# Linear-attention block with a dense expert layer on one core: key sums turned round, numerators kept transposed, denominators taken apart

## The chip, the cores and the metric

The kernel runs on one core of a Trainium2 chip. The metric is the device time of one execution in microseconds (us). Names of engines: PE is TensorE's matmul stream and PEld its weight loads, DVE is VectorE, ACT is ScalarE, POOL is GpSimd, SP is SyncE, which issues most of the transfers (DMAs).

## The reference, cut to what matters

All numbers are fp32. There are 2048 tokens of 512 features, 32 heads of 16 features, and 8 experts of 1792 hidden features.

```python
x = A_x
h = x + attention(layernorm(x))            # A
out = h + experts(layernorm(h))            # B

# attention: per head, features are two softmaxes of a small projection
phi_q = concat([softmax(pq), softmax(-pq)])        # 32 features a head
phi_k = concat([softmax(pk), softmax(-pk)])
kv  = einsum("bhsf,bhsd->bhfd", phi_k, v)          # sum over all tokens
z   = einsum("bhsf->bhf", phi_k)                   # sum over all tokens
num = einsum("bhqf,bhfd->bhqd", phi_q, kv)
den = einsum("bhqf,bhf->bhq", phi_q, z)[..., None] + 1e-6
o   = (num / den) @ wo

# experts: all 8 are used by every token (top 8 of 8), weighted by a softmax gate
h_  = gelu(einsum("nd,edf->nef", xt, w1))
y   = einsum("nef,efd->ned", h_, w2)
out = einsum("ne,ned->nd", cw, y)
```

The features phi_q and phi_k of a head are non-negative, and kv and z are needed in full before the first query can be answered.

## The kernel before, in words

Tokens are cut into 16 tiles of 128 (NT). A table STAGES lists stages as (lag, function); in step i, the stage with lag l works on tile i - l. The functions of one step are written in the order of the table, and the recording layer then sets the order of each engine's instructions from all of them; buffers are handed out by pools, so an instruction also waits for the last user of its buffer. SBUF pools are s4 (43 slots of 4 KB a partition) and s2 (13 slots of 2 KB); PSUM has 4 banks named ps and 4 named pacc.

For a tile of keys: x_stats and x_norm (layer norm: statistics on DVE, the power -0.5 on POOL, the subtraction and scaling on DVE, L157), x_trans (four PE transposes, L162), k_proj (two projections with the split fp32r product of L66 to L68, three matmuls for one), k_exp and k_feat (the softmaxes: maxima and minima L175 and L176, sums L182, reciprocals L183 on DVE, products L184 on POOL), and k_sum (L231). k_sum takes eight matmuls: the features of four heads (128) are the stationary operand, and the values of these heads with a column of ones behind each (4 x 17 = 68 columns) are the moving one. The sums of all tiles stay in two pacc banks. After the last tile keys_done (L272) masks the parts that belong to other heads.

For a tile of queries: q_proj, q_sub, q_exp, q_feat as above, q_trans (eight transposes, L262), q_num (L284: eight matmuls with the transposed features stationary and the 68 columns of kv moving, then on DVE the addition of 1e-6 L288, the reciprocal L289 and the product L290, all straight from PSUM), q_otrans (four transposes and the split into two fp32r parts), q_out (projection, residual, statistics of the second norm), q_norm, q_ntrans, and the gate: gate_parts (L333) multiplies with the gate weights in four column tiles of 32 side by side, chosen by tile_position.

From step END + 1 on, the expert layer is fed in between: hook runs four pieces of moe a step. Each quad there uses the four ps banks (L66 to L68 with ps), each down the pacc banks. From about 345 us to the end the expert layer alone fills PE.

Two lines carry the key sums and the numerators:

```python
nc.tensor.matmul(kvp[b][:, i * HN:(i + 1) * HN], phi[:, g * P:(g + 1) * P], v[:, g * HG:(g + 1) * HG, :]...)
nc.tensor.matmul(p[:, i * HN:(i + 1) * HN], phT[:, b * n + i, :], kv[:, b * n + i, :], start=True, stop=True)
```

## Time and profile before

| what | value |
|---|---|
| time, median of three runs | 2473.61 us (2472.48 to 2475.82) |
| time of the profiled execution | 2476.47 us |
| its span, first to last instruction | 2474.8 us |
| granted TensorE clock, mean | 0.995 |
| PE busy | 2449.9 us (99%) |
| DVE busy | 2159.9 us (87%) |
| ACT busy | 1757.4 us (71%) |
| POOL busy | 493.0 us (20%) |

The profile comes from one execution. "Busy" of PE is the union of the modelled spans of its matmuls, which overlap; how fast PE goes is therefore read from the starts of groups that follow each other, not from busy time or from the mean of one.

### The profile page before, as it was taken

The numbers are of one execution on the slowest core, as the hardware profiler recorded it, in microseconds if no ns is written. First come the engines' busy times: TensorE is split into PE (matmuls) and PEld (weight loads), VectorE is DVE, ScalarE is ACT, GpSimd is POOL, SyncE is SP. The second block draws the span as 40 slices with busy tenths as digits, with TensorE's granted clock in tenths as the row PEclk, the third lists the DMA queues.
The fourth block names the chain that finished last, engine by engine and source line by source line (L and its number), as shares of the span: only waits on it lengthen the run. The fifth ranks groups of instructions, "written<-read, shape, count | busy, mean of one in ns | idle before, by whom it ended". The sixth has DMA issues, their size and how long they took to land.

```text
span 2474.8 us, 32087 instructions
## 1 busy us (share of the span) xinstructions
PE 2449.9 (99%) x11272; PEld 2033.7 (82%) x11272; DVE 2159.9 (87%) x3204; ACT 1757.4 (71%) x2886; POOL 493.0 (20%) x562
## 2 busy tenths in 40 slices
PE   9999999999999999999999999999999999999998
PEld 8888778888888888888888888878888888888886
DVE  7677898988989989889896998889989889898987
ACT  4344477777777777777776777677777777777774
POOL 4565101111111111111111331111111111111120
PEclk9999999999999999999999999999999999999999
DMA  3001348787787787877877898887877887877785
GB/s 112 10 26 56 116 171 170 141 169 159 146 158 152 159 168 142 168 160 137 167 151 188 184 189 160 209 184 162 150 159 147 164 162 141 167 155 158 155 155 143
DMA packets 175202, 369.22 MB, mean 149 GB/s; under 512 B 15136, under 2 KB 81696, under 8 KB 175040
## 3 DMA queue, kind: packets, MB, share of 16 engines
q0 software_dynamic: 62304, 204.50, 49.6%
q1 hardware_dynamic: 111680, 162.62, 20.6%
q8 instruction: 88, 1.44, 0.2%
q14 instruction: 74, 0.61, 0.1%
q10 hardware_dynamic: 1056, 0.05, 0.0%
HBM read 158.38 MB, written 216.60 MB: 152 GB/s over the span
## 4 chain that ended last, share of the span: by engine, by line
PE 89%; DVE 4%; DMA 1%; issue 1%; POOL 1%; ACT 0%; SPq 0%; DVEq 0%; POOLq 0%; ACTq 0%
PE ps L66 15%; PE ps L67 15%; PE ps L68 15%; PE pacc L67 14%; PE pacc L68 14%; PE pacc L66 14%; PE ps L284 1%; DMA out_dram<-s 1%; DVE s L61 1%; DVE s L182 1%; PE pacc L162 1%; PE pacc L262 0%; POOL s L184 0%; DVE s L604 0%; DMA s<-in_B_w_dram 0%
## 5 line engine op out<-in xcount | busy, mean ns | idle before, releaser
L61 DVE TENSOR_TENSOR s<-s,s 128x512 fp32r<-128x512 f32 (+1 forms) x800 | 755.6, 958 | 158.7 <-ACT s L60 148.8
L60 ACT ACTIVATE s<-s 128x512 fp32r<-128x512 f32 (+1 forms) x800 | 669.7, 843 | 23.8 <-DVE s L511 8.7
L66 PE MATMUL pacc<-s,s 128*128 128x512 f32 x1732 | 678.1, 392 | 2.9 <-ACT s L60 2.9
L67 PE MATMUL pacc<-s,s 128*128 128x512 f32 x1732 | 675.7, 390 | 0.6 <-DVE s L61 0.6
L68 PE MATMUL pacc<-s,s 128*128 128x512 f32 x1732 | 675.6, 390 | 0.0
L66 PE MATMUL ps<-s,s 128*128 128x512 f32 x1664 | 652.3, 392 | 8.8 <-DVE ps L656 3.1
L67 PE MATMUL ps<-s,s 128*128 128x512 f32 x1664 | 649.2, 390 | 0.5 <-DVE s L61 0.5
L68 PE MATMUL ps<-s,s 128*128 128x512 f32 x1664 | 649.1, 390 | 0.0
L541 ACT ACTIVATE s<-pacc 128x512 f32<-128x512 f32 x742 | 440.2, 595 | 191.8 <-PE pacc L68 166.9
L603 ACT ACTIVATE ps<-ps 128x512 f32<-128x512 f32 x448 | 262.7, 587 | 190.3 <-DVE ps L656 119.0
L66 PEld LDWEIGHTS pacc<-s,s 128*128 128x128 f32 x1732 | 326.0, 188 | 71.9 <-ACT s L60 3.3
L67 PEld LDWEIGHTS pacc<-s,s 128*128 128x128 f32 x1732 | 326.1, 188 | 68.7 <-DVE s L61 1.9
L68 PEld LDWEIGHTS pacc<-s,s 128*128 128x128 f32 x1732 | 326.1, 188 | 68.0
L66 PEld LDWEIGHTS ps<-s,s 128*128 128x128 f32 x1664 | 313.1, 188 | 77.4 <-DVE ps L656 3.8
L67 PEld LDWEIGHTS ps<-s,s 128*128 128x128 f32 x1664 | 313.5, 188 | 65.0 <-DVE s L61 1.0
L68 PEld LDWEIGHTS ps<-s,s 128*128 128x128 f32 x1664 | 313.1, 188 | 65.3
L604 DVE TENSOR_TENSOR s<-ps,s 128x512 f32<-128x512 f32 x448 | 302.9, 685 | 50.7 <-ACT ps L603 47.1
L543 POOL DMA_DIRECT2D acc0m<-s x182 | 155.8, 856 | 822.9 <-ACT s L541 797.1
L543 POOL DMA_DIRECT2D acc1m<-s x175 | 150.4, 860 | 788.5 <-ACT s L541 766.9
L511 DVE TENSOR_TENSOR s<-s,s 128x1024 f32<-128x1024 f32 x220 | 268.1, 1219 | 0.1
L608 ACT ACTIVATE ps<-ps 128x512 f32<-128x512 f32 x226 | 132.1, 584 | 75.3 <-PE ps L68 75.3
L485 DVE TENSOR_TENSOR s<-s,s 128x1024 fp32r<-128x1024 f32 x112 | 136.2, 1216 | 0.0
(121 smaller groups left out, 1794.4 us busy)
## 6 DMA issues: line engine op xcount, KB each, us to landing
acc0m<-s POOLq DMA_DIRECT2D x192, 512.0 KB, 5.5
acc1m<-s POOLq DMA_DIRECT2D x182, 512.0 KB, 5.7
s<-in_B_w_dram SPq DMA_DIRECT2D x112, 512.0 KB, 5.2
s<-in_B_w_dram SPq DMA_DIRECT2D x224, 256.0 KB, 5.9
s<-in_A_x_dram SPq DMA_DIRECT2D x32, 256.0 KB, 2.7
s<-cwT SPq DMA_DIRECT2D x16, 512.0 KB, 5.1
h<-s SPq DMA_DIRECT2D x16, 256.0 KB, 2.0
s<-h SPq DMA_DIRECT2D x16, 256.0 KB, 5.6
```

What stands on the lines that cost most here:

```text
L60: nc.scalar.activation(hi, src, AF.Copy)
L61: eng.tensor_tensor(lo, src, hi.bitcast(F32), op=ALU.subtract)
L66: nc.tensor.matmul(out_, al, bh, start=first, stop=False, skip_group_check=True)
L67: nc.tensor.matmul(out_, ah, bl, start=False, stop=False, skip_group_check=True)
L68: nc.tensor.matmul(out_, ah, bh, start=False, stop=last, skip_group_check=True)
L485: nc.vector.tensor_tensor(sl, s, sh.bitcast(F32), op=ALU.subtract)
L511: nc.vector.tensor_tensor(B[out_], B[a], B[b], op=ALU.subtract)
L541: nc.scalar.activation(e[:, d], p[d], AF.Copy)
L543: nc.gpsimd.dma_start(macc[h, m], e, accum_op=ALU.add)
L603: nc.scalar.activation(src, src, AF.Gelu_apprx_tanh)
L604: nc.vector.tensor_tensor(B[b][:, q % 2], src, CW[h, e][:, int(b[2]) - 1], op=ALU.mult)
L608: nc.scalar.activation(dst, src, AF.Copy)
```

## The change

Three things change. (1) The layer norms are applied on ScalarE (one activation with a scale and a bias), for which GpSimd also makes the bias. (2) The key sums are turned: the values with their column of ones (two heads, 34 columns) are the stationary operand, the features of the two heads (64 columns) the moving one, in two column tiles of 64; they come a step later (k_feat lag 3, k_sum lag 4). When all keys are done, ScalarE copies the sums to SBUF, PE transposes them, and DVE masks kv and z apart. (3) A numerator has dimensions in partitions and tokens in columns: kv is stationary (64 columns), the transposed features move (128 columns), in two column tiles, and the result needs no transposes before the output projection. The denominators of four tiles are made together (q_den, 32 matmuls in four column tiles of 32), inverted, written to DRAM, and read back 16 times repeated by 16 transfers of 64 KB; DVE multiplies the numerators with them in PSUM. The table of stages is written anew, with one of its own (BEGIN) for the first five steps, and END falls from 25 + 8 to 24 + 8.

```diff
     def norm_stats(src, t):
...
+        nc.gpsimd.tensor_scalar(mv[:, t, 1:2], mv[:, t, 0:1], rs[:, t:t + 1], -1.0, op0=ALU.mult, op1=ALU.mult)
     def norm_apply(src, t):
         xn = s2()
-        nc.vector.tensor_scalar(xn, src, mv[:, t, 0:1], rs[:, t:t + 1], op0=ALU.subtract, op1=ALU.mult)
+        nc.scalar.activation(xn, src, AF.Identity, bias=mv[:, t, 1:2], scale=rs[:, t:t + 1])
...
     def k_sum(t):
         phi, v = st.pop(("f", t)), st.pop(("v", t))
-        for g in range(NG):
-            b, i = divmod(g, NG // 2)
-            nc.tensor.matmul(kvp[b][:, i * HN:(i + 1) * HN], phi[:, g * P:(g + 1) * P],
-                             v[:, g * HG:(g + 1) * HG, :].rearrange("p h d -> p (h d)"),
-                             start=(t == 0 and i == 0), stop=(t == NT - 1), skip_group_check=True)
+        for i in range(NG):
+            for c in range(2):
+                h = HG * (2 * (i // 2) + c) + HP * (i % 2)
+                nc.tensor.matmul(kvp[c * FW:c * FW + VW, i * FW:(i + 1) * FW],
+                                 v[:, h:h + HP, :].rearrange("p h d -> p (h d)"), phi[:, 2 * Dh * h:2 * Dh * (h + HP)],
+                                 start=(t == 0 and i == 0), stop=(t == NT - 1), tile_position=(0, c * FW),
+                                 skip_group_check=True)
+        if t == NT - 2:
+            st["kv"] = s2()
+            nc.gpsimd.memset(st["kv"], 0.0)
...
     def keys_done():
...
+        for c in range(2):
+            r = slice(c * FW, c * FW + VW)
+            nc.scalar.activation(kvs[r], kvp[r], AF.Copy)
+        z = st["z"] = s2((P, NG, 2 * DW))
+        nc.gpsimd.memset(z, 0.0)
+        p = ps()
+        for k in range(KD):
+            nc.tensor.transpose(p[:, k * P:(k + 1) * P], kvs[:, k * P:(k + 1) * P], ident)
...
+    def q_den(t):
+        c, j = divmod(t, TC)
+        if j < TC - 1:
+            return
+        p = ps_acc()
+        for j in range(TC):
+            phT = st["ph", c * TC + j]
+            for g in range(2):
+                a = ZP - (2 * j + g) * HG
+                for k in range(KD):
+                    nc.tensor.matmul(p[k * DW:(k + 1) * DW, :P], st["z"][:, 2 * k + g, a:a + DW], phT[:, 2 * k + g, :],
+                                     start=(j == 0 and g == 0), stop=(j == TC - 1 and g == 1),
+                                     tile_position=(0, k * DW), skip_group_check=True)
+        d = s2((P, P))
+        nc.vector.tensor_scalar(d, p[:, :P], 1e-6, None, op0=ALU.add)
+        nc.vector.reciprocal(d, d)
+        st["den", c] = [s4([P, KH, 512]) for _ in range(2)]
+        nc.sync.dma_start(rden[c], d)
+        src = rden[c].rearrange("(k j h) t -> h k j t", k=KD, h=2 * HG)
+        for i in range(2):
+            for h in range(2 * HG):
+                nc.sync.dma_start(
+                    st["den", c][i][h * Dh:(h + 1) * Dh].rearrange("p k (j t) -> p k j t", j=TC),
+                    src[h, i * KH:(i + 1) * KH].partition_broadcast(Dh))
...
     def q_num(t):
...
+        p = ps_acc()
+        for k in range(KD):
+            for g in range(2):
+                nc.tensor.matmul(p[g * FW:(g + 1) * FW, k * P:(k + 1) * P], kv[:, 2 * k + g, :], phT[:, 2 * k + g, :],
+                                 start=True, stop=True, tile_position=(0, g * FW))
...
+        for i in range(2):
+            k = slice(i * KH, (i + 1) * KH)
+            nc.vector.tensor_tensor(pv[:, k], pv[:, k], st["den", c][i][:, :, j * P:(j + 1) * P], op=ALU.mult)
...
+    BEGIN = [(1, k_proj), (-2, x_norm), (-1, x_trans), (-1, x_low), (4, k_sum), (2, k_exp), (-3, x_stats), (3, k_feat)]
...
+    END = 24 + HALF
```

The first place is PE at the end of the keys. In the lines below, L231 and L236 are the key sums of the last tile, L262 and L271 the transposes of query features, L284 the first numerators, L288 the transposes of the finished sums; ps and pacc are PSUM banks. Before:

```order
L231 MATMUL pacc_132<-s4_1447,s4_1503 128x68 x4
L231 MATMUL pacc_133<-s4_1447,s4_1503 128x68 x4
L262 MATMUL pacc_1587<-ident_69,s4_1478 128x128 x4
L262 MATMUL pacc_1593<-ident_69,s4_1478 128x128 x4
L66 MATMUL ps_1606<-s4_575,s4_707 128x512
...
L284 MATMUL ps_1629<-kv_134,s4_1373 128x68 x4
L284 MATMUL ps_1638<-kv_134,s4_1373 128x68 x4
```

And of the changed kernel, with the denominators of the first four tiles (L311):

```order
L236 MATMUL pacc_132<-s4_1635,s4_1543 34x64 x16
L271 MATMUL pacc_1789<-ident_69,s4_1646 128x128 x4
L271 MATMUL pacc_1795<-ident_69,s4_1646 128x128 x4
L288 MATMUL ps_1769<-ident_69,s2_1701 128x128 x4
L66 MATMUL ps_1802<-s4_575,s4_761 128x512
...
L311 MATMUL pacc_1820<-s4_1486,s2_1767 32x128 x8
```

Between the last key sums and the first use of kv or z stand, now as before, eight transposes and one projection of a query tile; four transposes of the sums are new there, and one query tile more (five instead of four) has been transposed by the end of it.

The second place is POOL at the same time. L184 and L185 are the products of the softmaxes, L245, L246, L254 and L255 the subtractions for a query tile, L221 and L222 that of a key tile. Before, from the last key tile's subtraction on:

```order
L221 TENSOR_TENSOR s4_1503<-mx_1500,s2_1419 128x32x16
L245 TENSOR_TENSOR s4_1540<-s2_1392,mx_1537 128x32x16
L184 TENSOR_TENSOR s4_1478<-s4_1478,s_1512 128x1024
L246 TENSOR_TENSOR s4_1540<-mx_1537,s2_1392 128x32x16
L184 TENSOR_TENSOR s4_1503<-s4_1503,s_1558 128x1024
```

Now, from the last key tile's product on:

```order
L185 TENSOR_TENSOR s4_1635<-s4_1635,s_1703 128x1024
L254 TENSOR_TENSOR s4_1710<-s2_1596,mx_1707 128x32x16
L255 TENSOR_TENSOR s4_1710<-mx_1707,s2_1596 128x32x16
L242 MEMSET s2_1701 128x512
L185 TENSOR_TENSOR s4_1646<-s4_1646,s_1713 128x1024
L254 TENSOR_TENSOR s4_1781<-s2_1666,mx_1778 128x32x16
L255 TENSOR_TENSOR s4_1781<-mx_1778,s2_1666 128x32x16
L185 TENSOR_TENSOR s4_1710<-s4_1710,s_1784 128x1024
L285 MEMSET s2_1767 128x512
```

The memset of z (L285) stands behind two more query tiles' subtractions and two products; the masks of z on DVE, and with them the first denominators, come after it.

The third place is DVE at the first denominators. L175 and L176 (now L176 and L177) are maxima and minima, L182 (now L183) sums, L61 the low part of a split weight. Before, the denominators of a tile and their product stand next to each other and take everything from PSUM:

```order
L288 TENSOR_SCALAR den_1634<-ps_1629 128x16
L183 RECIPROCAL s_1624<-s_1624 128x64
L289 RECIPROCAL den_1634<-den_1634 128x16
L288 TENSOR_SCALAR den_1643<-ps_1638 128x16
L290 TENSOR_TENSOR s2_1628<-ps_1629,den_1634 128x256
```

Now:

```order
L315 TENSOR_SCALAR s2_1853<-pacc_1820 128x128
L316 RECIPROCAL s2_1853<-s2_1853 128x128
L176 TENSOR_REDUCE mx_1972<-s2_1898 128x32
L177 TENSOR_REDUCE mx_1972<-s2_1898 128x32
L61 TENSOR_TENSOR s4_1913<-s4_1612,s4_1913 128x512
L183 TENSOR_REDUCE s_1923<-s4_1878 128x64
L339 TENSOR_TENSOR pacc_1927<-pacc_1927,s4_1856 128x256
L184 RECIPROCAL s_1923<-s_1923 128x64
```

L339 reads s4_1856, the first half of the repeated denominators, which comes back by DMA; four instructions of DVE stand between the reciprocal and it.

## Rows read from the trace of the kernel before

**Rows 1.** The page's first part: busy time, share of the span and instructions of an engine, after the span.

```profile
span 2474.8 us, 32087 instructions
PE 2449.9 (99%) x11272; PEld 2033.7 (82%) x11272; DVE 2159.9 (87%) x3204; ACT 1757.4 (71%) x2886; POOL 493.0 (20%) x562
```

**Rows 2.** Busy time by stretch: the stretch in us, its length, then busy time (and instructions) of PE, PEld, DVE, ACT and POOL, the granted TensorE clock, the DMA engines' share, and GB/s.

```profile
20.00:160.00 140.00, 140.00 (x806) 122.02 (x806) 104.03 (x168) 55.31 (x85) 75.98 (x72) 1.00 0.09 27
...
160.00:174.00 14.00, 11.72 (x54) 10.07 (x52) 7.55 (x17) 5.53 (x9) 9.64 (x7) 0.76 0.00 0
174.00:280.00 106.00, 105.93 (x695) 92.43 (x693) 85.45 (x221) 45.48 (x85) 47.96 (x41) 1.00 0.21 68
...
280.00:300.00 20.00, 17.53 (x87) 14.02 (x87) 19.90 (x40) 13.48 (x21) 1.21 (x2) 0.91 0.34 107
...
320.00:340.00 20.00, 17.35 (x80) 13.37 (x79) 20.00 (x32) 14.59 (x28) 2.36 (x3) 1.00 0.20 67
340.00:2400.00 2060.00, 2055.88 (x9086) 1699.78 (x9085) 1840.21 (x2598) 1569.54 (x2580) 341.98 (x406) 1.00 0.79 163
```

**Rows 3.** What PE waited for between 20 and 420 us: who, for whom, us in total, times, the longest.

```profile
PE pacc L231 <- POOL s L184: 2.3, 1, 2.3
PE pacc L162 <- DVE s L157: 2.1, 1, 2.1
PE ps L66 <- ACT ps L608: 1.9, 2, 1.1
PE ps L66 <- DVE s L485: 0.8, 1, 0.8
```

**Rows 4.** Groups of PE in order of time, two steps: start, length, line and operation, stationary x moving sizes, number of instructions.

```profile
156.84 1.90 PE L231 MATMUL pacc<-s,s 128*128 128x68 f32 x16
158.58 1.04 PE L262 MATMUL pacc<-ident,s 128*128 128x128 f32 x8
...
248.06 1.04 PE L162 MATMUL pacc<-ident,s 128*128 128x128 f32 x8
248.93 1.90 PE L284 MATMUL ps<-kv,s 128*128 128x68 f32 x16
250.67 1.04 PE L262 MATMUL pacc<-ident,s 128*128 128x128 f32 x8
```

**Rows 5.** Groups of instructions of the first 520 us by line and shape: count, busy us, mean ns of one, idle time before them.

```profile
L231 PE MATMUL pacc<-s,s 128*128 128x68 f32 x256 | 31.4, 277 | 2.3 <-POOL s L184 2.3
L231 PEld LDWEIGHTS pacc<-s,s 128*128 128x128 f32 x256 | 30.9, 196 | 2.9 <-POOL s L184 2.7
L284 PE MATMUL ps<-kv,s 128*128 128x68 f32 x256 | 30.5, 272 | 0.0
...
L333 PEld LDWEIGHTS pacc<-s,wg_pad 128*32 128x32 f32 x32 | 0.9, 108 | 1.4 <-ACT s L320 0.5 <-ACT s L541 0.4 <-ACT ps L603 0.2
```

**Rows 6.** Groups of PE in order of time around one gate_parts (L333, the column tiles that the kernel before already has). Its eight instructions stand as two lots of four.

```profile
345.03 0.39 PE L68 MATMUL ps<-s,s 128*128 128x512 f32 x1
345.35 0.64 PE L333 MATMUL pacc<-s,wg_pad 128*32 128x512 f32 x4
...
345.80 0.61 PE L333 MATMUL pacc<-s,wg_pad 128*32 128x512 f32 x4
346.34 0.50 PE L66 MATMUL ps<-s,s 128*128 128x512 f32 x1
346.68 0.39 PE L67 MATMUL ps<-s,s 128*128 128x512 f32 x1
346.91 0.39 PE L68 MATMUL ps<-s,s 128*128 128x512 f32 x1
```

**Rows 7.** DVE's groups by line and shape, 0 to 345 us, columns as in rows 5.

```profile
L182 DVE TENSOR_REDUCE s<-s 128x64 f32<-128x1024 f32 x32 | 38.6, 1216 | 19.6 <-ACT s L250 11.1 <-ACT s L222 8.5
L157 DVE TENSOR_SCALAR s<-s,mv,rs 128x512 f32<-128x512 f32 x32 | 23.6, 738 | 19.8 <-POOL rs L153 19.6
L150 DVE BATCH_NORM_STATS2 bn<-s 128x6 f32<-128x512 f32 x32 | 21.6, 675 | 6.6 <-DMA s<-in_A_x_dram 6.6
...
L183 DVE RECIPROCAL s<-s 128x64 f32<-128x64 f32 x32 | 16.9, 540 | 0.0
...
L290 DVE TENSOR_TENSOR s<-ps,den 128x256 f32<-128x256 f32 x32 | 12.5, 415 | 0.0
...
L289 DVE RECIPROCAL den<-den 128x16 f32<-128x16 f32 x32 | 6.6, 229 | 0.0
...
L288 DVE TENSOR_SCALAR den<-ps 128x16 f32<-128x16 f32 x32 | 4.8, 163 | 4.6 <-PE ps L284 3.9
```

**Rows 8.** POOL's groups, 0 to 345 us, columns as in rows 5.

```profile
L184 POOL TENSOR_TENSOR s<-s,s 128x1024 f32<-128x1024 f32 x32 | 62.5, 1957 | 74.8 <-DVE s L183 37.2 <-DVE rs L152 21.5 <-DVE den L289 4.4
...
L245 POOL TENSOR_TENSOR s<-s,mx 128x512 f32<-128x512 f32 x16 | 18.6, 1161 | 0.0
...
masks.py:197 POOL MEMSET ident<- 128x128 f32 x1 | 0.2, 204 | 0.3 <-POOLq L968 0.3
```

**Rows 9.** The page's DMA issues: transfer, queue, count, KB each, median us from issue to landing; and one line of the view of a source line: issues on SP's queue, ns (least, median, most).

```profile
s<-in_A_x_dram SPq DMA_DIRECT2D x32, 256.0 KB, 2.7
s<-cwT SPq DMA_DIRECT2D x16, 512.0 KB, 5.1
h<-s SPq DMA_DIRECT2D x16, 256.0 KB, 2.0
...
L457 SPq DMA_DIRECT2D s<-cwT x16: 326/338/408, 291.9 to 2254.4; - x16
```

More of the change, by code (lines that the diff above doesn't have):

```diff
@@ L185, in feat_norm @@
         return e.rearrange("p h s f -> p (h s f)")
-    kvp = [ps_acc() for _ in range(2)]
+    kvp = ps_acc()
     def x_norm(t):
@@ L263, in q_trans @@
             nc.scalar.activation(phT[:, b * n:(b + 1) * n, :], p.rearrange("p (i t) -> p i t", i=n), AF.Copy)
-    kv = consts.tile([P, NG, HN], F32, name="kv")
+    DW = P // KD
+    ZP = DW - HG
+    kv = consts.tile([P, NG, FW], F32, name="kv")
     def keys_done():
-        n = NG // 2
-        for b in range(2):
-            for i in range(n):
-                nc.vector.tensor_tensor(
-                    kv[:, b * n + i, :].rearrange("p (h d) -> p h d", h=HG),
-                    kvp[b][:, i * HN:(i + 1) * HN].rearrange("p (h d) -> p h d", h=HG),
-                    hmask.rearrange("p (h o) -> p h o", o=1).to_broadcast([P, HG, DE]), op=ALU.mult)
+        kvs = st.pop("kv")
+        for c in range(2):
[6 more added lines that the diff above has]
+            nc.tensor.transpose(p[:, k * P:(k + 1) * P], kvs[:, k * P:(k + 1) * P], ident)
+        pv = p.rearrange("p (g f) -> p g f", g=NG)[:, :, :VW].rearrange("p g (b d) -> p g b d", b=HP)
+        for a in range(HG // HP):
+            m = hmask[:, a * HP:(a + 1) * HP].rearrange("p (x b y) -> p x b y", x=1, y=1)
+            w = FW * HP // HG
+            nc.vector.tensor_tensor(kv[:, :, a * w:(a + 1) * w].rearrange("p g (b d) -> p g b d", b=HP),
+                                    pv[:, :, :, :Dh], m.to_broadcast([P, NG, HP, Dh]), op=ALU.mult)
+            nc.vector.tensor_tensor(z[:, :, ZP + a * HP:ZP + (a + 1) * HP], pv[:, :, :, Dh],
+                                    m[:, :, :, 0].to_broadcast([P, NG, HP]), op=ALU.mult)
@@ new lines, in block_kernel @@
+    rden = [dram.tile([P, P], F32, name=f"rden{c}") for c in range(NT // TC)]
+    def q_den(t):
[22 more added lines that the diff above has]
+                    src[h, i * KH:(i + 1) * KH].partition_broadcast(Dh))
@@ L277, in q_num @@
     def q_num(t):
         phT = st.pop(("ph", t))
-        o = st["o", t] = s2()
-        n = NG // 2
-        for b in range(2):
-            p = ps()
-            for i in range(n):
-                nc.tensor.matmul(p[:, i * HN:(i + 1) * HN], phT[:, b * n + i, :], kv[:, b * n + i, :],
-                                 start=True, stop=True)
-            nv = p[:, :n * HN].rearrange("p (h d) -> p h d", d=DE)
-            den = work.tile([P, H // 2, 1], F32, name="den")
-            nc.vector.tensor_scalar(den, nv[:, :, Dh:], 1e-6, None, op0=ALU.add)
-            nc.vector.reciprocal(den, den)
-            nc.vector.tensor_tensor(o[:, b * (D // 2):(b + 1) * (D // 2)].rearrange("p (h d) -> p h d", d=Dh),
-                                    nv[:, :, :Dh], den.to_broadcast([P, H // 2, Dh]), op=ALU.mult)
@@ L892, in block_kernel @@
     XA = 5
[L893 to L897 removed]
+    BEGIN = [(1, k_proj), (-2, x_norm), (-1, x_trans), (-1, x_low), (4, k_sum), (2, k_exp), (-3, x_stats), (3, k_feat)]
+    STAGES = [(14, q_exp), (-2, x_norm), (-1, x_trans), (-1, x_low), (1, k_proj), (17, q_den), (24, gate_parts),
+              (4, k_sum), (2, k_exp), (-3, x_stats), (3, k_feat), (13, q_sub), (14, q_feat), (21, q_num), (23, q_norm),
+              (15, q_trans), (22, q_out), (24, gate), (23, q_ntrans), (25, lambda t: gate_rows(t, 25)),
+              (27, lambda t: gate_rows(t, 27)), (11, q_proj)]
+    END = 24 + HALF
     late = {}
```

24 lines of the change are left out of this document (12 added, 12 removed).

## The prediction

> **What bounds the kernel now.** The page's busy times come first: PE 99%, DVE 87%, the rest less [rows 1]. They are a mean over stages, so the view by stretch is next: PE is busy without a break from 20 to 160 us, from 174 to 280, and nearly so from 340 on; it idles 2.3 us in 160 to 174, 2.5 in 280 to 300, 2.65 in 320 to 340 [rows 2]. The granted clock is 0.76 in the first of these stretches and 0.91 in the second, so the half level (1.2 GHz) cost 14 x 0.24 = 3.4 and 20 x 0.09 = 1.8 us more. The view of waits names the causes: POOL's softmax product for the last key sums (2.3), the norm on DVE (2.1), and ACT and DVE in the first expert pieces (1.9 and 0.8) [rows 3]. All else is PE's own pace, so the change is worth (a) what it takes from PE's stream and (b) what it does to these stalls. DVE, POOL and ACT count only where PE would wait for them.
>
> **PE's pace.** Key sums take 158.58 - 156.84 = 1.74 us a tile, numerators 250.67 - 248.93 = 1.74, eight transposes 248.93 - 248.06 = 0.87 [rows 4]. Each fp32 matmul is two instructions (256 for 128 matmuls [rows 5]), so one costs 0.109 us with 68 moving columns, as much as a transpose with 128: a load of 128 weight columns sets this pace, not the moving columns. A transpose gives 0.109/128 = 0.85 ns a column.
>
> The column tiles are the unknown, and gate_parts is the only row of them: four instructions start together at 345.35, the other four at 345.80 [rows 6]. So four tiles do run side by side, and the second instruction of a tile follows the first after 0.45 us for 512 columns: 0.435 at 0.85 ns, and some 20 ns on top. Entering and leaving cost: 345.35 - 345.03 less the usual 0.23 (346.91 - 346.68) is 0.09; 346.34 - 345.80 less 0.435 is 0.10; the next matmul is 0.11 late (346.68 - 346.34 less 0.23). Together 0.30 us a visit [rows 6]. The Trainium skill says the same of the cause, and it speaks against this change, which makes 36 such visits: TensorEngine Tiling (Array Packing), Key Properties, says that a change of tiling mode drains the engine. The trace agrees, with these 0.30 us; without them the sum below would be 36 x 0.30 = 10.8 us lower.
>
> **Sum on PE**, with 0.85 ns a column + 20 ns an instruction, tiles side by side:
> - Key sums: 8 matmuls x 2 = 16 instructions of 64 columns a tile, 16 x 0.074 + 0.30 = 1.49 for 1.74: saves 0.25 x 16 tiles = 4.0.
> - Numerators: 8 of 128 columns, 8 x 0.129 + 0.30 = 1.33; away go 1.74 and four transposes (0.44): saves 0.85 x 16 = 13.6.
> - Denominators: new, 16 of 128 columns in each of four tiles, 16 x 0.129 + 0.30 = 2.36, four times: costs 9.4.
> - Four transposes of the sums: costs 0.4.
> That is -7.8 us. Bounds: were weight loads hidden wholly, the 20 ns would go: 1.17, 1.17 and 2.04 us, so -9.1 - 16.2 + 8.2 + 0.4 = -16.7. Did two tiles of 64 not run side by side at all, key sums would be 32 x 0.074 + 0.30 = 2.67 and numerators 16 x 0.129 + 0.30 = 2.36: +14.9 + 2.9 + 9.4 + 0.4 = +27.6. I take -7.8, the pace of the row.
>
> **The norms.** 32 x 738 ns = 23.6 us leave DVE, and with them 19.6 us in which DVE stood waiting for POOL's power [rows 7]; ACT gets 32 instructions and that wait. POOL's bias, 128x1, is bounded by its own power (596 ns, of the same size) and nothing. I give all this no price on PE outside the two late stalls: PE there waits for neither. Cover lost: if ACT, standing for POOL, copied projections out late, PE would stand for a PSUM bank.
>
> DVE gets lighter in all: per tile two additions, reciprocals and products (2 x (163 + 229 + 415) = 1614 ns) become two products (830) and a quarter of an addition and a 128x128 reciprocal (2 x 540 [rows 7] + some 250 = 1330, a quarter 330).
>
> **The stall at the end of the keys (5.7 us with its clock).** The key sums now stand a step behind the products on POOL, so the old wait should go. What is late next: the first denominators need z, whose memset stands behind two more query tiles on POOL. From the last key product to it: four subtractions of 1.16, two products of 1.96, two memsets of some 0.6 (0.204 for a quarter of the size) [rows 8] = 9.8 us, then 1.2 for the masks on DVE. PE has until then 1.49 + 0.87 + 0.44 + 12 x 0.23 = 5.6 us. So up to 5.4 us of stall are here again, for 5.7 that go. Taken: 0, between -5.7 and +5.4.
>
> **The stalls at 280 to 340 us (6.9 us).** The 2.1 behind DVE's norm, and the 1.8 of clock, should go with the norm from DVE; of the 2.65 later, in which DVE is busy 20.00 of 20 [rows 2], half (1.3). Taken: -5.2; between -6.9 and 0.
>
> **The repeat through DRAM.** It adds a wait in DVE's queue. From the last matmul of q_den: 0.25 + 1.1 for addition and reciprocal; 0.33 + 2.0 for the write (h<-s); eight issues of 0.34 and 2.7 to land (the x tiles) [rows 9]: the first half is there after 9.1 us. The second eight wait each for the transfer eight before, on the same semaphore: 12 us. SP's queue holds residual loads and h stores behind these 17 issues; none is needed within a step. Behind L339 in DVE's queue stand the softmax sums of the next query tiles and the next products, which PE needs. PE's stock in the new order, from q_den to the first row that needs DVE behind the wait:
> - tiles 0 to 3: four query projections were brought forward; about 20 us against some 16 needed. No stall.
> - tiles 4 to 7: 15.2 us to the next transposes of features (needed 13.1 + 1.96 on POOL = 15.1), 16.1 to q_out, needed 18.6 (5.5 us of DVE rows of 0.4 to 0.7 further): 2.5 late.
> - tiles 8 to 11: the same count gives 1.8 late.
> - tiles 12 to 15: expert pieces stand between; none.
> Taken: +4.3. Bounds: 0, if DVE has run ahead, and the next paragraph's price.
>
> Sum: -7.8 + 0 - 5.2 + 4.3 = -8.7. From the profiled execution, 2476.5 (2474.8 of span and 1.7 around it), this gives 2467.8; it stood 2.9 above the median of the three runs, so **2465**.
>
> **Rivals.**
> *The repeated denominators come late (slower).* One mechanism: landing takes 5.1 us, as the other repeated read does (s<-cwT) [rows 9], not 2.7. Each half is 2.4 later, and the second half waits for the first, so 4.8. From where PE's stock is used up, in three of the four groups of tiles, PE stands 4.8 longer, and the clock falls to its half level with it, as it did after the idle time in 160 to 174 (3.4 us [rows 2]). Price: 4.3 + 3 x (4.8 + 3.4) = 28.9 in place of 4.3, so 2465 + 24.6 = 2490. For it: 512-byte pieces, a queue in order. Against: a transfer is only 64 KB, and few others run then (DMA share 0.21).
> *Weight loads cost by the column.* Loads of 32 and 128 columns last 108 and 196 ns [rows 5]: 0.9 ns a column, and gate_parts' 20 ns could be the load of its 32 columns. Then 34 columns cost 31 and 64 columns 58 ns with each instruction: 1.66, 1.63 and 2.5 us, so -1.3 - 8.7 + 10 + 0.4 = +0.4 on PE, and 2465 + 8.2 = 2473. The Trainium skill has such a rule: TensorE: Matmul & The Clock Gate, Part 3, The mechanism, lets a weight load overlap a running matmul only where row groups differ, and column tiles share theirs. One shape in the trace cannot tell this from a fixed price.
> *Loads hidden, stalls gone.* PE -16.7, late stalls -6.9, no wait for DMA: 2476.5 - 23.6 - 2.9 = 2450.
> *The end of the keys costs more.* The 5.4 us come on top, as the clock falls with it: 2470.
> *The change doesn't do what it says:* two tiles of 64 in turn: 2465 + 27.6 + 7.8 = 2500. The four tiles of 32 speak against it.
>
> **How the numbers follow.** 0.2% (5 us) is about what a measurement can tell from no change. Forecast 0.40, its own range 2459 to 2471; loads hidden 0.18; loads by the column 0.14; denominators late 0.14; end of keys 0.10; in turn 0.04. Faster (below 2468.6): 0.35 + 0.18 + 0.02 + 0.04 + 0.01 = 0.60; slower (above 2478.6): 0.03 + 0.11 + 0.04 = 0.18; the rest, 0.22, is no change. 2448 to 2483 leaves the last case out, and most of the denominators' case.
>
> **What would show it.** Start to start, a tile's key sums should take about 1.5 us with the visit, its numerators 1.3, a group's denominators 2.4; 1.65, 1.63 and 2.5 would mean loads by the column, over 2.3 for the first two tiles in turn. PE's waits should no longer name the norm; a wait of DVE (L339) for the repeated denominators should stand in DVE's list with some 4 to 6 us a group, and little of it in PE's. Idle time of PE between q_den and q_out of the second and third group would mean the slower rival; a wait of L311 for DVE or POOL, the end of the keys. The prediction is wrong at its root if PE stands idle in 174 to 280 us by more than 8 us.

## The result, and the profile after

The changed kernel takes 2495.59 us (median of four runs, 2494.79 to 2497.55) beside 2474.72 for the kernel before: ratio 1.0087, interval 1.0075 to 1.0099. It is 21 us slower; the forecast was 2465, its range ended at 2483.

The page's first part, for [rows 1]:

```profile
span 2494.6 us, 33097 instructions
PE 2444.1 (98%) x11724; PEld 2010.2 (81%) x11724; DVE 2142.7 (86%) x3112; ACT 1777.7 (71%) x2920; POOL 506.2 (20%) x596
```

PE is busy 5.8 us less and idle 25.6 us more (2494.6 - 2444.1 = 50.5 for 24.9); together they are the 19.8 us of the span. Busy time by stretch, columns as in [rows 2]:

```profile
20.00:160.00 140.00, 137.44 (x1074) 112.69 (x1073) 101.17 (x161) 64.82 (x100) 83.12 (x88) 1.00 0.08 24
160.00:174.00 14.00, 8.00 (x58) 6.32 (x57) 9.30 (x15) 7.25 (x12) 11.56 (x10) 0.67 0.00 1
174.00:280.00 106.00, 87.70 (x694) 68.33 (x693) 62.61 (x124) 44.32 (x80) 42.51 (x43) 0.93 0.29 88
280.00:300.00 20.00, 16.69 (x170) 12.75 (x166) 13.77 (x32) 9.95 (x18) 3.41 (x6) 1.00 0.39 110
300.00:320.00 20.00, 17.44 (x81) 13.10 (x81) 15.55 (x27) 10.33 (x16) 0.81 (x2) 0.83 0.46 148
320.00:340.00 20.00, 20.00 (x113) 15.36 (x110) 14.94 (x37) 14.20 (x25) 2.14 (x4) 1.00 0.42 139
340.00:2400.00 2060.00, 2055.80 (x9090) 1699.15 (x9090) 1842.81 (x2605) 1569.72 (x2582) 345.73 (x407) 1.00 0.80 162
```

From 340 to 2400 us PE's busy time does not differ. In 174 to 280 us, where PE had stood 0.07 us, it stands 18.3, and no engine took its place: DVE, ACT and POOL are busy 62.61, 44.32 and 42.51 us of 106, less than before (for DVE in part because the change took work from it). Each stands for the others, as the lists below show. The clock adds to it: by an estimate from these rows (busy time x the share that was not granted) the half level (1.2 GHz) costs 8.00 x 0.33 + 87.70 x 0.07 + 17.44 x 0.17 = 11.7 us of busy time between 160 and 340 us, for 11.72 x 0.24 + 17.53 x 0.09 = 4.4 before.

What PE waited for between 20 and 420 us, for [rows 3]:

```profile
PE pacc L66 <- DVE s L61: 5.8, 2, 3.6
PE pacc L271 <- ACT s L272: 5.4, 3, 2.7
PE ps L288 <- ACT s L283: 4.2, 1, 4.2
PE pacc L163 <- DVE s L348: 4.0, 3, 2.3
PE pacc L271 <- POOL s L185: 3.9, 2, 2.0
PE pacc L163 <- ACT s L158: 2.7, 2, 1.4
PE pacc L271 <- ACT s L212: 2.6, 1, 2.6
```

Short waits for nearly every stage of the query side, none for a DMA: no single late thing, but a chain without slack. The new products themselves, groups of PE in order of time (columns as in [rows 4]):

```profile
94.95 1.09 PE L236 MATMUL pacc<-s,s 128*34 128x64 f32 x32
95.97 0.50 PE L66 MATMUL ps<-s,s 128*128 128x512 f32 x1
...
202.88 1.09 PE L332 MATMUL pacc<-s,kv 128*64 128x128 f32 x16
203.91 1.09 PE L271 MATMUL pacc<-ident,s 128*128 128x128 f32 x8
...
284.71 0.60 PE L163 MATMUL pacc<-ident,s 128*128 128x128 f32 x4
285.24 1.95 PE L311 MATMUL pacc<-s,s 128*32 128x128 f32 x64
287.13 1.09 PE L332 MATMUL pacc<-s,kv 128*64 128x128 f32 x16
288.15 0.50 PE L66 MATMUL pacc<-s,s 128*128 128x512 f32 x1
```

Start to start, key sums take 95.97 - 94.95 = 1.02 us, numerators 1.03, a group's denominators 1.89, and 285.24 - 284.71 less four transposes (0.44) gives 0.09 for entering: 1.11, 1.12 and 1.98 a visit. That is a saving of 16 x (1.74 - 1.11) = 10.1 for the key sums and 16 x (2.18 - 1.12) = 17.0 for the numerators, and a cost of 7.9 + 0.4: 18.8 us less in PE's stream, not 7.8. So some 40 us are lost elsewhere; PE's idle time (25.6 more) and the clock (7.3 more) hold 33 of them, and the rest isn't placed. What it looks like in DVE's list about the first two tiles of numerators:

```profile
184.69 1.22 DVE L183 TENSOR_REDUCE s<-s 128x64 f32<-128x1024 f32 x1 [0.26 <-ACT s L259]
187.45 0.43 DVE L339 TENSOR_TENSOR pacc<-pacc,s 128x256 f32<-128x256 f32 x1 [1.54 <-DMA s<-rden]
187.79 0.54 DVE L184 RECIPROCAL s<-s 128x64 f32<-128x64 f32 x1
188.25 1.16 DVE L183 TENSOR_REDUCE s<-s 128x64 f32<-128x1024 f32 x1
195.56 0.43 DVE L339 TENSOR_TENSOR pacc<-pacc,s 128x256 f32<-128x256 f32 x1 [6.15 <-PE pacc L332]
195.90 0.54 DVE L184 RECIPROCAL s<-s 128x64 f32<-128x64 f32 x1
```

The landing of the repeat (DMA s<-rden) held DVE 1.54 us. The next multiplication (195.56) waited 6.15 for the second tile's numerators, and the reciprocal for the next query features stood behind it. In all DVE waited 15.0 us for late numerators in 160 to 340 us; before, the like wait (L288 for L284) was 3.9.

```profile
DVE pacc L339 <- PE pacc L332: 15.0, 7, 6.2
```

Why PE was late with them is in PE's order:

```
L332 MATMUL pacc<-s_1486,kv 64x128 x8
L271 MATMUL pacc<-ident,s_1781 128x128 x4
L66 MATMUL ps<-s_575,s_913 128x512
...
L68 MATMUL ps<-s_675,s_1154 128x512
L271 MATMUL pacc<-ident,s_1781 128x128 x4
L332 MATMUL pacc<-s_1583,kv 64x128 x8
```

Between the first and the second tile's numerators stand 48 products (L66 to L68, the four query projections of s_913 to s_1154): 183 to 194 us. Before, twelve stood there. From the third tile on this projection is missing as a filler: in the fifth to the ninth tile 24 products stood before the numerators in the kernel before, and 20, 17 and then 12 stand before those of the fifth, sixth and later tiles now.

### The profile page after: what moved, and what is told of

The parts are those of the page before. It is cut to its first block, busy times and chain, and to the rows that moved or that the text cites. A ratio compares the mean times of both kernels' runs of the same rounds, so it can differ in the third digit from the quotient of the medians.

```text
span 2494.6 us, 33097 instructions
## 1 busy us (share of the span) xinstructions
PE 2444.1 (98%) x11724; PEld 2010.2 (81%) x11724; DVE 2142.7 (86%) x3112; ACT 1777.7 (71%) x2920; POOL 506.2 (20%) x596
## 4 chain that ended last, share of the span: by engine, by line
PE 86%; DVE 3%; POOL 2%; issue 2%; ACT 1%; DMA 1%; SPq 0%; DVEq 0%; POOLq 0%; ACTq 0%
PE ps L66 14%; PE ps L67 14%; PE ps L68 14%; PE pacc L67 14%; PE pacc L66 14%; PE pacc L68 14%; POOL s L185 1%; DVE s L183 1%; DVE s L61 1%; DMA out_dram<-s 1%; PE pacc L332 0%; PE pacc L271 0%; POOL s L254 0%; POOL s L255 0%; ACT s L60 0%
## 5 line engine op out<-in xcount | busy, mean ns | idle before, releaser
L61 DVE TENSOR_TENSOR s<-s,s 128x512 fp32r<-128x512 f32 (+1 forms) x800 | 756.6, 959 | 159.0 <-ACT s L60 148.9
L66 PE MATMUL pacc<-s,s 128*128 128x512 f32 x1732 | 680.6, 393 | 9.7 <-DVE s L61 5.8
L60 ACT ACTIVATE s<-s 128x512 fp32r<-128x512 f32 (+1 forms) x800 | 669.1, 842 | 19.6 <-DVE s L556 9.0
L68 PE MATMUL pacc<-s,s 128*128 128x512 f32 x1732 | 677.7, 391 | 0.0
L66 PE MATMUL ps<-s,s 128*128 128x512 f32 x1664 | 652.9, 392 | 4.2 <-DVE ps L701 2.6
L68 PE MATMUL ps<-s,s 128*128 128x512 f32 x1664 | 649.5, 390 | 0.0
L66 PEld LDWEIGHTS pacc<-s,s 128*128 128x128 f32 x1732 | 327.0, 189 | 79.4 <-DVE s L61 6.9
L68 PEld LDWEIGHTS pacc<-s,s 128*128 128x128 f32 x1732 | 327.6, 189 | 68.7
L66 PEld LDWEIGHTS ps<-s,s 128*128 128x128 f32 x1664 | 313.6, 189 | 71.7 <-DVE ps L701 3.0
L68 PEld LDWEIGHTS ps<-s,s 128*128 128x128 f32 x1664 | 313.5, 188 | 65.6 <-issue 0.2
```

Of the source, the lines that this page charges most:

```text
L60: nc.scalar.activation(hi, src, AF.Copy)
L61: eng.tensor_tensor(lo, src, hi.bitcast(F32), op=ALU.subtract)
L66: nc.tensor.matmul(out_, al, bh, start=first, stop=False, skip_group_check=True)
L68: nc.tensor.matmul(out_, ah, bh, start=False, stop=last, skip_group_check=True)
```

## The experiments

Times are medians; "before" ran between 2473.8 and 2475.7 beside them.

**e1_num_ps, e2_norm_dve, e3_no_repeat, e4_trans_ps: one part of the changed kernel undone each.**

```diff
 # e1, in q_num            # e4: the same in q_trans
-        p = ps_acc()
+        p = ps()
 # e2, norm_apply, without GpSimd's bias
-        nc.scalar.activation(xn, src, AF.Identity, bias=mv[:, t, 1:2], scale=rs[:, t:t + 1])
+        nc.vector.tensor_scalar(xn, src, mv[:, t, 0:1], rs[:, t:t + 1], op0=ALU.subtract, op1=ALU.mult)
 # e3, in q_den, in place of all transfers
+        st["den", c] = [st["one"], st["one"]]
```

> Edit: the numerators take a bank named ps instead of pacc. Three theories for the 21 us: BANKS (transposes of features, numerators, output projections, transposes of the norm and the gate all share four pacc banks, while the four ps banks stand empty from about 200 to 320 us; PE stands because a bank is not yet read out), NORM (ACT's queue stands behind the norm, which waits for POOL, and everything ACT copies out comes late), REPEAT (the denominators come back late through DRAM). BANKS expects over half of the stall of 160 to 360 us gone: 2455 to 2475 us, and PE's waits on bank readers L272, L61 and L348 under 6 us in sum. NORM and REPEAT expect 2490 to 2500 us.

> Edit: the norms are applied on DVE again, as before the change, and POOL makes no bias. NORM expects 2460 to 2480 us, and the waits of PE on ACT's copies L272 and L283 mostly gone. BANKS and REPEAT expect 2490 us or more, as DVE gets its 24 us of work and its waits for POOL back.

> Edit: the denominators are made and inverted, but not written to DRAM nor read back; DVE multiplies by a constant tile of ones of the same shape, so the division is left out of the output. REPEAT expects 2465 to 2480 us. BANKS and NORM expect 2488 to 2498 us, as DVE waited for these transfers for 5 us only.

> Edit: the transposes of the query features take ps banks instead of pacc. BANKS expects 2450 to 2475 us, at least as much as for the numerators, since the transposes take two banks a tile. NORM and REPEAT expect 2490 to 2500 us.

Measured: 2485.1, 2482.4, 2471.6 and 2486.7 us (ratios 1.0044, 1.0030, 0.9988, 1.0049; the intervals 0.0010 to 0.0015 either way). In e3 the division is left out. The 24 us of e3 are what REPEAT expected; e1, e2 and e4 (10.5, 13.2 and 8.9 us) lie between their theories. Each part has a share, and the repeat has the largest, though DVE waits for its transfers only 5.0 us in 160 to 360 us:

```profile
DVE s L524 <- DMA s<-rden: 2.7, 1, 2.7
DVE pacc L339 <- DMA s<-rden: 2.3, 2, 1.5
```

Only the second line is the multiplication; L524 belongs to the expert layer. That e1 and e4 change the order too (twelve products between the first tiles' numerators) means that their banks and their order aren't told apart. e2 keeps the 48 products in a row and most of PE's idle time in 174 to 280 us (17.0), so most of what it gives lies outside that stretch:

```profile
174.00:280.00 106.00, 89.02 (x674) 70.00 (x676) 70.97 (x135) 39.51 (x75) 38.49 (x34) 0.92 0.30 92
```

**e5_untied, e9_two_loads: what in the repeat.** e5 cuts the tie of the transfers to the denominators, e9 keeps buffers and bytes but makes two transfers of sixteen, from the input too. Both leave the division out.

```diff
 # e5
-        src = rden[c].rearrange("(k j h) t -> h k j t", k=KD, h=2 * HG)
+        src = x[c * P:(c + 1) * P, :P].rearrange("(k j h) t -> h k j t", k=KD, h=2 * HG)
 # e9, the only reads
+            nc.sync.dma_start(st["den", c][i].rearrange("p k t -> p (k t)"),
+                              x[(2 * c + i) * 2 * P:(2 * c + i + 1) * 2 * P, :].rearrange("(p a) d -> p (a d)", a=2))
```

> The changed kernel, with the sixteen repeating transfers of each four tiles reading a fixed block of the input x (rows and columns of the same shape) instead of the denominators' block; the denominators are still computed, inverted and written, the transfers still fill the same two s4 buffers, and VectorE still multiplies by them. So the numerators are multiplied by numbers that are not the denominators: the division is left out. Theory CHAIN (numerators stand for denominators that land late: reciprocal, write, read back): about 2472, as with the whole repeat gone (2471.6). Theory ROOM (the two s4 buffers and the seventeen transfers themselves, which take places and a queue from the rest): about 2493 to 2497, as the changed kernel. Theory ORDER (the order of the instructions, which the planner writes round the transfers and which is nearly the same here): also 2490 to 2497; it is told from ROOM by another run.

> The changed kernel, in which two transfers of 512 KB from the input x fill the two s4 buffers of each four tiles, where sixteen of 64 KB repeated the denominators (the denominators are still computed, inverted and written; the division by them is left out). The buffers and the bytes stay as they are; the number of transfers falls from 17 to 3, and with it PE's order: after the first tile's numerators stands one projection of 12 products, where the changed kernel has 48 products in a row before the second tile's numerators, and later tiles have a second projection between them again, as without the repeat. Theory ORDER (the 48 products in a row let VectorE, ScalarE and GpSimd stand and leave PE without filler work after 200 us; the planner put them there for the transfers): about 2472 to 2476. Theory ROOM (two s4 buffers less for the rest): about 2493 to 2497.

Measured: e5 2496.4 (1.0087), e9 2474.4 (0.9997, 0.9988 to 1.0007). Untying gives nothing, though PE's waits move: in e5 the 48 products stand one tile later, and PE waits for the norm of ScalarE (L158).

```profile
PE pacc L163 <- ACT s L158: 16.4, 4, 6.8
```

Fewer transfers, with the same buffers and bytes, give 21 of the 24 us. The theory ROOM falls. In e9's PE order twelve products stand between the first two tiles' numerators. PE's row for 174 to 280 us, and DVE's wait for numerators (L329 there):

```profile
174.00:280.00 106.00, 97.63 (x861) 76.30 (x859) 75.92 (x153) 52.70 (x95) 47.02 (x47) 0.99 0.31 104
...
DVE pacc L336 <- PE pacc L329: 2.0, 1, 2.0
```

861 instructions for 694, at a clock of 0.99, and 2.0 us of waiting for 15.0. e9 has larger pieces besides fewer transfers; as no engine but DVE waited for a transfer in the changed kernel (5.0 us), the order is what is left, by elimination.

**e6_all_three, e7_before_keysums, e8_before_norm_act: are the parts separate costs and gains?** e6 joins e1, e2 and e3. e7 and e8 put one part of the change into the kernel before:

```diff
 # e7, in k_sum (with keys_done as in the change, kv as before)
+                nc.tensor.matmul(kvp[c * FW:c * FW + VW, i * FW:(i + 1) * FW],
+                                 v[:, h:h + HP, :].rearrange("p h d -> p (h d)"), phi[:, 2 * Dh * h:2 * Dh * (h + HP)],
 # e8, in norm_apply (with GpSimd's bias)
+        nc.scalar.activation(xn, src, AF.Identity, bias=mv[:, t, 1:2], scale=rs[:, t:t + 1])
```

> The changed kernel with three edits at once: no repeat through DRAM (VectorE multiplies by a constant tile of ones; the division is left out), the numerators' sums in the ps banks instead of pacc, and the normalisations back on VectorE. Alone they gave -24, -10.5 and -13 us. Theory SUM (three separate costs): 2495.6 - 47 = about 2448, where the matmul stream alone, some 22 us shorter than before's, would put it. Theory SHARED (all three only give slack to the same few steps, PE short of work between 200 and 320 us): 2463 to 2472, little under the best one.

> The kernel before with the turned key sums alone (values as the weights, 32 products of 34 to 64 columns in two column tiles, the transposes and masks at the end of the keys); order of stages, normalisations and the whole query side as before. By the changed kernel's trace a tile's key sums take about 1.1 us on PE for 1.74, sixteen times: -10 us. Theory LOCAL: the stream's gain arrives, less the stall at the end of the keys (4 to 6 us, a copy on ScalarE late): 2466 to 2471. Theory ABSORBED (what the key sums give is lost again while PE waits for the feature maps' engines in 20 to 160 us, or at the end of the keys): 2473 to 2477. Slower than 2477 would speak for a stall at the end of the keys larger than the gain.

> The kernel before with the normalisations alone moved to ScalarE (GpSimd makes the bias, ScalarE applies scale and bias). Theory NORM (a normalisation that stands in ScalarE's list behind GpSimd's bias holds up the copies that free PE's banks, whatever else is changed): slower by 8 to 14 us, 2483 to 2489. Theory SHARED (this costs only where PE is already short of work and banks, as in the changed kernel): 2472 to 2478.

Measured: e6 2469.6 (0.9981), e7 2478.1 (1.0014, 1.0004 to 1.0024), e8 2476.2 (1.0005, 0.9996 to 1.0015). The three are shared, not summed. e7 is the surprise: ten us less in PE's stream, and the kernel is some 4 us slower, a little above what ABSORBED allowed; that speaks, as was expected for over 2477, for a stall at the end of the keys. Its trace says where they went. DVE's rows of one key tile, first of the kernel before, then of e7:

```profile
102.55 0.55 DVE L157 TENSOR_SCALAR s<-s,mv,rs 128x512 f32<-128x512 f32 x1 [2.02 <-POOL rs L153]
106.36 1.22 DVE L182 TENSOR_REDUCE s<-s 128x64 f32<-128x1024 f32 x1 [0.87 <-ACT s L222]
110.79 0.55 DVE L157 TENSOR_SCALAR s<-s,mv,rs 128x512 f32<-128x512 f32 x1 [2.61 <-POOL rs L153]
```

```profile
102.60 0.55 DVE L157 TENSOR_SCALAR s<-s,mv,rs 128x512 f32<-128x512 f32 x1 [2.03 <-POOL rs L153]
106.41 1.22 DVE L182 TENSOR_REDUCE s<-s 128x64 f32<-128x1024 f32 x1 [0.87 <-ACT s L222]
110.84 0.55 DVE L157 TENSOR_SCALAR s<-s,mv,rs 128x512 f32<-128x512 f32 x1 [2.62 <-POOL rs L153]
```

A key tile goes round a loop of DVE and POOL in 8.24 us in both, to 0.05 us, as do the four before it, though e7's PE has less to do. In the kernel before PE is full beside it, with products that aren't due yet; in e7 it gets further ahead with them and stands when they are used up:

```profile
20.00:160.00 140.00, 136.63 (x1056) 112.25 (x1054) 101.64 (x168) 53.76 (x86) 76.41 (x73) 0.99 0.09 27
160.00:174.00 14.00, 9.34 (x71) 8.54 (x71) 7.77 (x13) 6.10 (x9) 8.62 (x6) 0.76 0.01 1
...
PE pacc L235 <- POOL s L184: 7.0, 2, 5.1
```

This wait, at the last two key tiles, was 2.3 before.

**e10_four_loads, e11_lag1, e12_four_num_norm: the division kept, with eight transfers; or a step more between denominators and numerators.**

```diff
 # e10, in q_den: the write by four transfers that put (j t) together, then
+        src = rden[c].rearrange("(k h o j) t -> k h o (j t)", k=KD, j=TC, o=1)
+        for k in range(KD):
+            nc.sync.dma_start(st["den", c][k // KH][:, k % KH, :], src[k].to_broadcast([2 * HG, Dh, 512]))
 # e11 (the changed kernel); e12 is e10 with e1 and e2
-(21, q_num), (23, q_norm)
+(22, q_num), (24, q_norm)
```

> The changed kernel with the whole division: the reciprocals are written in another order by four transfers, so that each of four reads, one for each 128 dimensions, takes runs of 2 KB and repeats them over 16 partitions (8 transfers for 17). PE's order then has 12 products between the first and the second tile's numerators, not 48. Theory ORDER: 2474 to 2482, most of the repeat's 24 us given back with the division in place. Theory ROOM, or one by which the repeat's bytes or latency cost the time: 2490 to 2497.

> The changed kernel with numerators, output projection, second normalisation, gates and what follows one step later (lags 22, 23, 24, 25, 26, 28 for 21 to 27), so that a step more lies between the denominators and their use. In PE's order 55 products then stand in a row before the first tile's numerators, and one projection a tile after them. Theory ORDER: no gain, 2492 to 2502. Theory LATENCY (the numerators come a step too early for the transfers): 2475 to 2485.

> Three edits that keep the whole computation: the repeat by eight transfers as in the run before, the numerators' sums in the ps banks, and the normalisations on VectorE. Theory SHARED (all that was lost is PE short of work between 200 and 320 us; the key phase is set by a loop of VectorE and GpSimd that the turned key sums don't touch): 2464 to 2474, as the kernel without the repeat with the same edits (2469.6), a few us above or below. Theory SUM (separate costs): about 2450. If ROOM or the repeat's bytes cost the time after all: 2480 or more.

Measured: 2485.8 (1.0043), 2491.5 (1.0068), 2485.5 (1.0041). e10 lies between its theories. e11 is half a microsecond under ORDER's range and far from LATENCY's. e12 lies above its first two theories and in the range of the third (ROOM or the repeat's bytes), which e13 below rules out: same bytes, 18 us less. In e10 the order is mended, and the landing is now late: what DVE waited for in 160 to 340 us, in e10,

```profile
DVE pacc L338 <- DMA s<-rden: 19.5, 7, 4.6
```

and 19.5 in e12 as well, for 5.0 in the changed kernel. In the changed kernel PE's order was so late that the transfers were mostly hidden behind it (DVE's 15.0 us for numerators).

**e13_four_early, e14_17_early: the denominators a step earlier, with eight and with seventeen transfers.**

```diff
 # both; e13 is built on e10, e14 on the changed kernel
-(1, k_proj), (17, q_den), (24, gate_parts), (4, k_sum), (2, k_exp)
+(1, k_proj), (24, gate_parts), (4, k_sum), (16, q_den), (2, k_exp)
```

> The changed kernel with the repeat by eight transfers (as e10_four_loads) and the denominators a step earlier (lag 16 for 17, behind the key sums in the step's list), with the whole division. In e10 VectorE stood 19.5 us in seven waits for the repeated denominators and PE stood 6.2 and 4.3 us at the third and fourth group; PE's order has no block of projections longer than 18 products here either. Theory LATENCY LEFT (of the 24 us, the order around the transfers takes some 13 and their landing after the numerators the other 11): 2472 to 2478, and VectorE's wait for the repeated denominators under 6 us. Theory ROOM LEFT (the eleven us are the buffers held, or the bytes moved): 2483 to 2490.

> The changed kernel with its seventeen transfers and nothing changed but the denominators a step earlier (lag 16). The transfers have a step more to land, but in PE's order 60 products stand in a row before the first tile's numerators, and one projection a tile after them. Theory ORDER: 2488 to 2500, no better than the changed kernel by more than a few us, and VectorE waits little for the transfers. Theory LATENCY alone: 2472 to 2480, as e13.

Measured: e13 2467.5 (0.9965, 0.9951 to 0.9979), e14 2488.7 (1.0058, 1.0043 to 1.0073). e13 is faster than both its theories, with the short wait that LATENCY LEFT named; e14 is where ORDER put it. With the changed kernel and e10 these make a square:

| | denominators at lag 17 | at lag 16 |
|---|---|---|
| seventeen transfers | 2495.6 | 2488.7 |
| eight transfers | 2485.8 | 2467.5 |

The window 174 to 280 us and DVE's waits for DMA, e13 and then e14:

```profile
174.00:280.00 106.00, 98.38 (x806) 77.59 (x805) 77.01 (x157) 55.05 (x99) 45.98 (x48) 0.98 0.36 113
...
DVE pacc L338 <- DMA s<-rden: 1.9, 1, 1.9
```

```profile
174.00:280.00 106.00, 86.42 (x662) 68.38 (x665) 63.73 (x125) 47.19 (x86) 44.91 (x44) 0.94 0.31 95
...
DVE pacc L339 <- DMA cwT<-row: 2.8, 1, 2.8
```

In e14 nothing waits for the repeated denominators any more, and PE still stands 19.6 us in this stretch. This points to the order as what the seventeen transfers cost (66 products stand between the first denominators and the first numerators here), and to the landing as what the eight of e10 cost. No run changed the order and nothing else, so the first half of this is argued.

**e15_four_early_norm, e16_four_early_norm_dvecopy, e17_idle_transfers, e18_old_keysums: what is left.**

```diff
 # e15: e13 with e2's edit    # e16: e15, in keys_done
-            nc.scalar.activation(kvs[r], kvp[r], AF.Copy)
+            nc.vector.tensor_copy(kvs[r], kvp[r])
 # e17: e13, behind the reads; nobody reads idle
+                nc.sync.dma_start(idle[i][h * Dh:(h + 1) * Dh].rearrange("p k (j t) -> p k j t", j=TC),
+                                  osrc[h, i * KH:(i + 1) * KH].partition_broadcast(Dh))
 # e18: e15 with k_sum of the kernel before, masks straight from its banks
+            nc.tensor.matmul(kvp[b][:, i * HN:(i + 1) * HN], phi[:, g * P:(g + 1) * P],
```

> As e13, with the normalisations back on VectorE; the whole computation. On the changed kernel this edit gave 13 us, on the kernel before it gave nothing (2476.2 for 2473.8 with the normalisations on ScalarE). Theory SHARED (it counts only where PE has run out of filler work): within 4 us of e13. Theory NORM (a cost of its own): 8 to 13 us under e13.

> As e15, with the two copies of the key sums out of PSUM at the end of the keys on VectorE instead of ScalarE, where they stand behind an exponential that waits for GpSimd (in the changed kernel PE's transposes wait 4.2 us for them, and the granted clock falls to 0.74 in the 20 us after). Theory END (this stall and the lower clock behind it cost their own time): 3 to 8 us under e15. Theory SHARED (the query features set the pace there anyway, GpSimd above all): within 2 us of e15.

> As e13 (eight transfers, denominators a step earlier: 2467.5), and behind each four reads the sixteen old 64 KB transfers once more on the same queue, into a block of DRAM that nobody reads. No engine waits for them, and no buffer is held for them. In PE's order, though, the second projection of a tile moves forward again: 26 and 19 products stand in a row about the third tile's numerators, and from the fifth on one projection a tile. Theory ORDER (the planner counts seventeen transfers as a long occupation of the queue and writes PE's order round them): 2480 to 2492. Theory LATENCY (what costs is a wait for the denominators' landing): 2466 to 2471, since nothing waits for these.

> As e15 (2465.1), with the key sums of the kernel before (features as the weights, 8 products of 68 columns a tile, two PSUM banks, masks read straight from PSUM; no copy, no transposes at the end of the keys). Numerators, denominators, stages and the repeat by eight transfers stay. PE's stream grows by about 10 us. Theory ABSORBED (in the key phase PE waits for the loop of VectorE and GpSimd whatever the key sums take, and gives back what it gained before 130 us between 130 and 165): 2462 to 2469. Theory LOCAL (the ten us of the stream come back): 2472 to 2478.

Measured: e15 2465.1 (0.9962, 0.9947 to 0.9977), e16 2468.6 (0.9975, 0.9966 to 0.9984), e17 2486.2 (1.0048, 1.0033 to 1.0063), e18 2467.7 (0.9977, 0.9967 to 0.9986).

- e15: where the order is mended, the normalisations' 13 us are gone (2.3 left, inside the spread). They were no cost of their own.
- e16 doesn't try what it should: the copy stands behind another instruction on DVE, and PE waits longer for it (5.6 us for 3.8 in e15), not less. What the stall at the end of the keys costs stays open.

```profile
PE ps L287 <- DVE s L282: 5.6, 1, 5.6
```

- e17: four times sixteen transfers that nobody reads cost 19 us. PE's order goes back to one projection a tile, and PE is busy 88.92 of the 106 us. It is no pure case of order, though: DVE waits 8.1 us for DMA behind the longer queue.

```profile
174.00:280.00 106.00, 88.92 (x718) 69.63 (x717) 65.21 (x129) 47.67 (x86) 43.91 (x44) 0.95 0.38 124
...
DVE pacc L345 <- DMA s<-rden: 4.6, 2, 3.0
DVE pacc L345 <- DMA idle<-rden: 3.5, 1, 3.5
```

- e18: with the old key sums the kernel is as fast within what can be told (2.6 us slower by the medians). Most of the ten us that the turned ones save on PE is absorbed: the loop of DVE and POOL takes 7.6 us a key tile in both, and at the end of the keys e15 stands for the copy where e18 does not. What remains of the change's gain comes with the numerators, the denominators and the new table together. 160 to 174 us, e15 and then e18:

```profile
160.00:174.00 14.00, 11.24 (x108) 9.18 (x108) 8.44 (x17) 5.91 (x12) 9.00 (x9) 0.88 0.03 8
160.00:174.00 14.00, 13.41 (x138) 11.57 (x137) 7.79 (x15) 3.64 (x6) 10.11 (x8) 1.00 0.01 2
```

## Why the prediction was wrong

**The step that failed** is the one on PE's stock in "The repeat through DRAM". It counted the four query projections that the order brings forward as cover ("about 20 us against some 16 needed. No stall"). They are the trouble: in an order that is fixed, forty-eight products in a row are also a delay of 11 us for what stands behind them, the second tile's numerators, and DVE stood for those (6.15 us; 15.0 in all, for 2.0 in e9). And a projection used up at 190 us isn't there at 240 (12 products before the seventh tile's numerators, for 24 before), where it had filled PE's time while features were made. I read the new order for what is there at the wait, not for what is missing after it. The wait itself was sized too high (2.3 us at L339 and 5.0 on DVE in all, for 4 to 6 a group), and its price too low: +4.3 for 21 to 24, by e9 and e3. That the price goes with the number of transfers (and the size of their pieces), and not with the landing, the buffers or the bytes, is shown by e5 and e9; that it comes by the order is argued from the orders and the waits.

**At its root:** "PE stands idle in 174 to 280 us by more than 8 us" was the sign that I had set; it stands 18.3. "DVE, POOL and ACT count only where PE would wait for them" held for the kernel before. It did not hold once 0.6 us a key tile was taken from PE: in e7 a loop of DVE and POOL, hidden before at 8.24 us a key tile, comes up as 7.0 us of PE's waiting for POOL.

**The sum on PE** was wrong in the good direction: -18.8 for -7.8. The term of 20 ns an instruction isn't there. 32 instructions of 64 columns go in 1.02 us, and 16 lots of 64 x 0.85 ns are 0.87: two tiles run side by side and their loads are hidden; 0.24 a visit are left for entering and leaving. That bound (-16.7) stood in the prediction, and I took the pace of the one row, -7.8. The 0.11 by which the next product is late was charged to the visit as well, but the old key sums had most of it too (63.19 - 62.87 = 0.32 for 0.23, behind the key sums at 61.17 us in the kernel before). Of the rivals on loads, the one by columns is refuted: 1.65 and 1.63 would have been seen for 1.11 and 1.12. It had behind it a sentence of the Trainium skill (TensorE: Matmul & The Clock Gate, Part 3, The mechanism: loads overlap only where row groups differ). Here column tiles of the same rows hid their loads, so the measurement decides against it. The Trainium skill also says (TensorEngine Tiling (Array Packing), Key Properties) that a change of tiling mode drains the engine. The trace agrees, with these 0.24 us.

**The norms at nothing** was right in the kernel before (e8: 2.3 us of 2474, not told from none) and in the mended one (e15), and wrong by 13 in between (e2): a price that depends on how much PE has to do meanwhile. The sentence on lost cover, ACT's copies late and PE without a bank, is what [rows 3]'s counterpart shows: L271 stands for the copies of L272 and L212 (8.0 us). But PE also stands for the norm itself, now ACT's L158 (2.7 us at L163), where its waits should no longer have named the norm; in e5 this wait is 16.4 us.

**The end of the keys at 0** (-5.7 to +5.4): PE stands 6.0 us in 160 to 174 for 2.3, with a clock of 0.67 for 0.76. The wait for POOL's products only moved (L271 for L185, 1.8), and the late thing was the copy L283 (4.2), in ACT's list behind an exponential that waits for POOL, not z's memset. **The stalls of 280 to 340 at -5.2:** the wait for DVE's norm at 284 us went, but PE stands 3.3 and 2.6 us in 280 to 320 for the split of DVE (L61: 5.8), 5.9 us in 280 to 340 for 5.1 before.

**The rival on the slower side** forecast the size (2490), by luck: its mechanism, a late landing, was not at work. The changed kernel's transfers landed in 2.9 us, and in e5 untying them changed nothing. The same mechanism was real one step on, in e10, where the order no longer hid it.

**A version that beats both:** e15, 2465.1 us, 0.38% (0.23 to 0.53) under the kernel before, is the change with eight transfers, denominators at lag 16 and normalisations on DVE. That is the number forecast, by another kernel and by luck: the terms of the sum did not come out.

## What to carry to other kernels

Before a stream of the fullest engine is shortened, look for the loop beside it that takes as long: if another engine's period doesn't follow, the gain ends as a stall further on (ten us of key sums, of which nothing clear of the noise reached the time in e7 and e18). Where a change alters the order, read it for fillers that are used up early as well as for the wait that they cover. And where a part costs more than the waits that name it, vary its number, bytes, buffers and dependence one by one, with the order printed beside each: here fewer transfers gave 21 us where untying gave nothing, and once they were fewer, making them a step earlier gave 18.

## What the runs showed of the hardware

Column tiles of 32 and of 64 columns hide their weight loads: 32 instructions of 64 columns in two tiles take 1.02 us start to start with leaving (16 lots of 0.054 and 0.15), 64 instructions of 128 columns in four tiles 1.89 (16 lots of 0.109 and 0.15). An fp32 instruction with 128 weight columns took 0.109 us with 68 moving columns and with 128 alike [rows 4]; in these column tiles the time went with the moving columns. And the clock fell about the longest stall: 0.67 in 160 to 174 us, where PE stands 6.0 us, 0.88 in e15 (2.8 us) and 1.00 in e18 (0.6). Not all idle time does this: in 280 to 300 us of e7 PE stands 4.1 us, and the clock is 1.00 there and in the next 20 us.
